# Rounding fp64 weights inside an attention + FFN kernel: the clamp on VectorE, a third of each weight while x arrives, the rest later

## Chip, cores, metric

One core of a Trainium2 chip. The metric is the device time of one execution in microseconds (us). Each time of a kernel below is a median of several executions with their range; what happens at which microsecond inside a kernel is read from its one profiled execution. PE is TensorE's matmuls, PEld its weight loads, DVE VectorE, ACT ScalarE, POOL GpSimd, SP SyncE.

## The reference, cut to what matters

```python
B, N, m, C = 4, 12416, 32, 128              # x [B,N,C] fp32, inducing points [m,C] fp32
h   = mab(inducing, x)                      # softmax(inducing x^T / sqrt(C)) x
att = mab(x, h)                             # each token of x attends to the 32 rows of h
xn  = att / rms(att) * rms_g                # 49664 tokens of 128
out = (silu(xn @ w_gate) * (xn @ w_val)) @ w_out      # d_ff = 1536; the weights are fp64
```

The three weights are fp64, 128 x 1536 words each. The kernel reads them as pairs of 32-bit words and rounds them to fp32 by integer steps: exponent out of the high word, clamped to what fp32 has, shifted into place; mantissa likewise; sign and low word joined in; one product. Each weight is cut into three chunks of 128 x 512, called (i,c): i = 0 gate, 1 val, 2 out; c = 0, 1, 2 the third.

## The kernel before

The FFN runs in slots of 128 hidden channels (12 slots make a unit of 512 tokens): gate matmul, val matmul, SiLU, multiply, and out projection two slots later. The next batch's attention is laid between the slots. Only batch 0's attention and the rounding of the weights stand ahead of the first slot; this part is called the head.

Some words for it. A *score group* is the scores of one piece of x against h. The FFN takes the attention weights themselves as input, so h is folded into the gate and val weights: a *stack* is the product of h with one third of such a weight, copied by ScalarE, with a subtraction on VectorE behind the copy. *gram* is the product of h with itself; from it comes each token's mean square. The *seam* is the chain that makes the attention weights of one piece ready for the FFN: product with gram, transposed back (z), reduced, the power (1/rms, on GpSimd), the scaling by it, a split into a high and a low part, and four small transfers (the gather).

The rounding of one chunk (cut):

```python
def load_w(i, c):
    ...
    def parts():
        ve.tensor_scalar(out=e[:], in0=high, scalar1=20, scalar2=0x7FF, op0=ALU.logical_shift_right, op1=ALU.bitwise_and)
        nc.gpsimd.tensor_scalar(out=e[:], in0=e[:], scalar1=896.0, scalar2=1151.0, op0=ALU.max, op1=ALU.min)   # the clamp, L211
        nc.scalar.activation(e[:], e[:], AF.Copy, bias=-896.0 * (1 << 23), scale=float(1 << 23))               # L212
        ve.tensor_scalar(out=f[:], in0=high, scalar1=0xFFFFF, scalar2=None, op0=ALU.bitwise_and)
        nc.scalar.activation(f.bitcast(F32)[:], f[:], AF.Copy, bias=1.0, scale=2.0 ** -20)                     # L214
    def join():
        ve.scalar_tensor_tensor(...)          # sign into e
        ve.scalar_tensor_tensor(...)          # low word into f
        nc.gpsimd.tensor_tensor(out=dst, in0=f.bitcast(F32)[:], in1=e.bitcast(F32)[:], op=ALU.mult)
        put()                                 # store the chunk for later batches, fetch the next raw chunk
```

The order of the work ahead of the first slot (cut); `convert` does the next half of a chunk:

```python
for s in range(NS):                    # 7 pieces of x
    for k in range(R): f["turn_x"](s, k)          # transposes; copies on ScalarE, each second one on VectorE
    if s: f["scores1"](s - 1); convert()
...
f["exp2"](0, 1); convert()
turn_a(); square()                     # square also turns z back
for i in range(2): f["stack_of"](i, 0) # matmul, ScalarE copy, VectorE subtraction
scale(); convert(3)
for c in range(1, NC):
    for i in range(2): f["stack_of"](i, c)
apply(); split(); gather(0, 0); convert(3)
# slots 0 and 1: the last two convert()
```

## Time and profile before

| | before |
|---|---|
| time, median of 4 (range) | 1759.96 us (1759.11 to 1761.65) |
| span of the profiled execution | 1759.6 us |
| PE, DVE, ACT, POOL busy | 97%, 65%, 44%, 11% |
| first FFN matmul | 83.05 us after the start |
| slot 9 starts | 103.33 us |

The first two rows are whole executions; the last two are read from the timeline of the profiled one. They matter because from about slot 9 on TensorE has hardly any gaps (from 118 us to the end it waits 4.3 us in all), so a microsecond won ahead of that slot is won at the end. The other views of this profile are shown in the prediction.

### The profile page before, as it was taken

What the parts mean: (1) busy time and instruction counts of PE and PEld (TensorE: products, weight loads), DVE (VectorE), ACT (ScalarE), POOL (GpSimd) and SP (SyncE); (2) the same over time, 40 slices, a digit from 0 to 9 for tenths busy, and PEclk for the clock granted to TensorE, in tenths of its full rate; (3) what the DMA queues carried; (4) which work ended last, traced back from release to release, by engine and by line L of the source; (5) the groups of instructions that cost most, each with busy time, mean ns of one, the idle gap of its engine ahead of it and who ended that gap; (6) DMA issues with size and microseconds to landing.
All of it is one profiled execution on the core that took longest, in us unless ns stands there. A gap on an engine that the chain in (4) does not pass through costs nothing.

```text
span 1759.6 us, 20237 instructions
## 1 busy us (share of the span) xinstructions
PE 1707.2 (97%) x6234; PEld 955.4 (54%) x6234; DVE 1144.2 (65%) x1982; ACT 769.0 (44%) x1288; POOL 188.4 (11%) x135
## 2 busy tenths in 40 slices
PE   6499999999999999999999999999999999999998
PEld 4245555555565555554556555555456555555555
DVE  4567765666567776566666777666656666666655
ACT  4244445333544444533454444534354444444444
POOL 2411100102111001011010010110101101100100
PEclk9699999999999999999999999999999999999999
DMA  6235363124343226113425315413211121121111
GB/s 252 66 67 86 54 144 68 42 66 75 56 76 67 51 54 147 36 42 90 69 51 90 54 30 112 100 28 80 49 31 36 28 42 25 31 42 33 27 35 23
DMA packets 389338, 112.44 MB, mean 64 GB/s; under 512 B 365136, under 2 KB 369776, under 8 KB 386672
## 3 DMA queue, kind: packets, MB, share of 16 engines
q1 hardware_dynamic: 388944, 111.02, 30.7%
q8 instruction: 49, 0.80, 0.2%
q14 instruction: 57, 0.47, 0.1%
q10 hardware_dynamic: 288, 0.15, 0.0%
HBM read 53.95 MB, written 27.00 MB: 46 GB/s over the span
## 4 chain that ended last, share of the span: by engine, by line
PE 92%; ACT 3%; DVE 2%; POOL 1%; issue 1%; DMA 1%; SPq 0%; DVEq 0%; ACTq 0%; POOLq 0%
PE acc L480 55%; PE gv L496 15%; PE gv L498 15%; PE mm L265 2%; PE mm L428 1%; PE mm L319 1%; ACT silu L500 1%; POOL u L211 1%; PE gv L265 1%; DMA xn<-in_x_dram 1%; ACT L500 1%; ACT sc L294 0%; PE gv L319 0%; ACT sc L367 0%; PE mm L380 0%
## 5 line engine op out<-in xcount | busy, mean ns | idle before, releaser
L480 PE MATMUL acc<-u,wo 128*128 128x512 f32 (+2 forms) x2400 | 1200.1, 583 | 0.3
L502 DVE TENSOR_TENSOR u<-silu,gv 128x512 f32<-128x512 f32 (+2 forms) x1200 | 798.5, 670 | 561.3 <-ACT silu L500 555.4
L500 ACT ACTIVATE silu<-gv 128x512 f32<-128x512 f32 (+2 forms) x1200 | 699.5, 584 | 926.7 <-DVE u L502 507.1
L496 PE MATMUL gv<-a,sg 128*128 128x512 f32 (+2 forms) x1200 | 922.4, 769 | 10.9 <-DMA a<-lo 8.1
L480 PEld LDWEIGHTS acc<-u,wo 128*128 128x128 f32 x2400 | 440.4, 188 | 151.0 <-issue 58.5
L498 PE MATMUL gv<-a,sv 128*128 128x512 f32 (+2 forms) x1200 | 465.8, 388 | 1.9 <-ACT silu L500 1.3
L496 PEld LDWEIGHTS gv<-a,sg 128*128 128x128 f32 x1200 | 227.5, 190 | 287.3 <-issue 272.4
L498 PEld LDWEIGHTS gv<-a,sv 128*128 128x128 f32 x1200 | 228.1, 190 | 275.4 <-issue 194.6
L431 POOL TENSOR_TENSOR z<-z,sc 128x512 f32<-128x512 f32 (+2 forms) x27 | 32.0, 1186 | 1043.3 <-DVE z L430 1022.8
L439 POOL TENSOR_TENSOR rs<-ms,mhalf 128x16 f32<-128x16 f32 (+2 forms) x28 | 75.9, 2711 | 116.6 <-DVE ms L437 116.6
L483 DVE STREAM_TRANSPOSE o<-acc 128x512 f32<-128x512 f32 (+2 forms) x100 | 69.1, 691 | 1.5 <-PE acc L480 1.1
L360 POOL TENSOR_TENSOR sc<-sc,mx 128x512 f32<-128x512 f32 (+2 forms) x24 | 23.2, 968 | 311.7 <-DVE mx L359 253.8
L245 DVE STREAM_TRANSPOSE xT<-xT 128x512 f32<-128x512 f32 (+2 forms) x84 | 53.2, 633 | 0.0
L428 PE MATMUL mm<-eT,gram 128*128 128x512 f32 (+2 forms) x56 | 28.4, 589 | 5.0 <-DVE eT L420 5.0
L443 POOL TENSOR_TENSOR sc<-sc,rs 128x512 f32<-128x512 f32 (+2 forms) x27 | 26.4, 976 | 2.1
L212 ACT ACTIVATE u<-u 128x512 int32<-128x512 int32 x9 | 5.7, 630 | 39.3 <-POOL u L211 39.3
L211 POOL TENSOR_SCALAR u<-u 128x512 int32<-128x512 int32 x9 | 18.2, 2018 | 35.3 <-DVE u L210 35.1
L253 PE MATMUL gv<-ident,xn 128*128 128x128 f32 x97 | 15.6, 326 | 5.9 <-ACT xT L259 3.5
L430 DVE STREAM_TRANSPOSE z<-mm 128x512 f32<-128x512 f32 (+2 forms) x28 | 18.6, 666 | 3.9 <-PE mm L428 3.9
L265 PE MATMUL mm<-xT,hT 128*32 128x512 f32 (+2 forms) x150 | 20.9, 592 | 0.0
L319 PE MATMUL mm<-xn,e 128*32 128x128 f32 x582 | 20.7, 276 | 0.0
L265 PE MATMUL mm<-xT,indT 128*32 128x512 f32 (+2 forms) x168 | 20.0, 547 | 0.0
(127 smaller groups left out, 445.5 us busy)
## 6 DMA issues: line engine op xcount, KB each, us to landing
out_dram<-o SPq DMA_DIRECT2D x320, 64.0 KB, 2.0
xT<-in_x_dram SPq DMA_DIRECT2D x60, 256.0 KB, 4.8
xn<-in_x_dram SPq DMA_DIRECT2D x60, 256.0 KB, 5.9
a<-hi SPq DMA_DIRECT2D x160, 64.0 KB, 2.0
a<-lo SPq DMA_DIRECT2D x158, 64.0 KB, 2.0
w<-w SPq DMA_DIRECT2D x21, 256.0 KB, 3.2
xn<-in_x_dram SPq DMA_DIRECT2D x5, 1024.0 KB, 11.6
out_dram<-o SPq DMA_DIRECT2D x64, 60.0 KB, 2.0
```

The lines of the kernel that those rows point to most:

```text
L211: nc.gpsimd.tensor_scalar(out=e[:], in0=e[:], scalar1=896.0, scalar2=1151.0, op0=ALU.max, op1=ALU.min)
L245: nc.vector.transpose(out=t[:, ts(k, n * m)], in_=t[:, ts(k, n * m)])
L265: nc.tensor.matmul(ps[ts(q, m), 0:w], lhsT, xT[b, s][:, ts(q, w)], start=True, stop=True)
L319: nc.tensor.matmul(ps[ts(t % R, m), 0:C], e[:, ts(t, m)], xn[:, t, :], start=head and t < R, stop=not more)
L428: nc.tensor.matmul(ps[rows, 0:w], gram[b][rows, rows], st["eT"][rows, 0:w], start=True, stop=True)
L439: nc.gpsimd.tensor_tensor(out=rs, in0=ms, in1=mhalf[rows, 0:n], op=ALU.pow)
L480: nc.tensor.matmul(acc[:, 0:T], wo[:, j, :], t[:, 0:T], start=(j == 0), stop=(j == NJ - 1))
L483: nc.vector.transpose(out=o[:, 0:T], in_=acc[:, 0:T])
L496: nc.tensor.matmul(g[:, 0:T], sg[:, ts(j, P)], a[:, 0:T], start=True, stop=True)
L498: nc.tensor.matmul(v[:, 0:T], sv[:, ts(j, P)], a[:, 0:T], start=True, stop=True)
L500: nc.scalar.activation(sl[:, 0:T], g[:, 0:T], AF.Silu)
L502: nc.vector.tensor_tensor(out=t[:, 0:T], in0=sl[:, 0:T], in1=v[:, 0:T], op=ALU.mult)
```

## The change

Intent: less work and fewer waits between engines ahead of the first slot. In parts:

1. The clamp goes from GpSimd to VectorE. While x arrives, the "place" steps (L212, L214) are done on VectorE too, and ScalarE has all copies of x.
2. Chunks are taken by thirds: only (0,0), (1,0), (2,0) while x arrives; (0,1), (1,1), (0,2) in gaps of the attention chain; (1,2), (2,1), (2,2) in slots 0 to 6.
3. Within the attention chain: scores against h ahead of the gram product, gram's copies on ScalarE, the stack's subtraction split from its copy and set behind the seam's reduction, the first FFN unit gathered before the stacks of the second third, the exponentials to h in four instructions instead of seven.
4. In the full part: some steps move by a few slots. Batch 0's remaining score groups begin seven slots later, so that by slot 9 one is done instead of three.

The core of the diff, cut:

```diff
-    chunks = [(i, c) for i in range(3) for c in range(NC)]
+    chunks = [(i, c) for c in range(NC) for i in ((0, 1, 2) if not c else (0, 1))] + [(2, c) for c in range(1, NC)]
...
-            nc.gpsimd.tensor_scalar(out=e[:], in0=e[:], scalar1=896.0, scalar2=1151.0, op0=ALU.max, op1=ALU.min)
+            nc.vector.tensor_scalar(out=e[:], in0=e[:], scalar1=896.0, scalar2=1151.0, op0=ALU.max, op1=ALU.min)
...
+        def place(scalar):
+            ...
+                    if scalar:
+                        nc.scalar.activation(to[:], t[:], AF.Copy, bias=add, scale=mul)
+                    else:
+                        nc.vector.tensor_scalar(out=to[:], in0=t[:], scalar1=mul, scalar2=add, op0=ALU.mult, op1=ALU.add)
...
-                if k == 1:
-                    nc.vector.tensor_copy(out=dst, in_=src)
-                else:
-                    nc.scalar.copy(out=dst, in_=src)
+                nc.scalar.copy(out=dst, in_=src)
...
+    early = [(step, i) for i in range(3) for step in (parts, join)]     # while x arrives: third 0
...
+    parts(1, 1)
+    place(1, 1)
     for i in range(2):
         f["stack_of"](i, 0)
+    turn_z()
     scale()
+    for i in range(2):
+        f["stack_low"](i, 0)
+    join(1, 1)
-    convert(3)
-    for c in range(1, NC):
-        for i in range(2):
-            f["stack_of"](i, c)
     apply()
     split()
     gather(0, 0)
+    parts(0, 2); place(0, 2)
+    for i in range(2):
+        f["stack_of"](i, 1); f["stack_low"](i, 1)
+    join(0, 2)
...
+            for k, step in enumerate((parts, place, join)):
+                add(k // 2, step, 1, NC - 1)                  # slots 0, 0, 1
+            for i in range(2):
+                add(2 + i, f["stack_of"], i, NC - 1)
+                add(2 + i, f["stack_low"], i, NC - 1)
+            for c in range(1, NC):
+                for k, step in enumerate((parts, place, join)):
+                    add(2 * c + 1 + k // 2, step, 2, c)       # slots 3, 3, 4 and 5, 5, 6
```

## The prediction

> **What bounds the kernel now.** I read the page first, then the stretches of the head, then the waits there, then the timeline around the two longest gaps. The page: slices of 44 us, then the chain that ended last.
>
> ```profile
> PE   6499999999999999999999999999999999999998
> PEclk9699999999999999999999999999999999999999
> ...
> PE 92%; ACT 3%; DVE 2%; POOL 1%; issue 1%; DMA 1%; SPq 0%; DVEq 0%; ACTq 0%; POOLq 0%
> ```
>
> TensorE is full from the third slice on, at full clock. From 118 us to the end its matmuls wait 4.3 us in all (the waits of PE in that window). That part is bound by TensorE's work, which the change leaves alone, so nearly all there is to win or lose lies in the two weak slices. Stretches of these (span, busy of PE, PEld, DVE, ACT, POOL; clock; DMA share; GB/s):
>
> ```profile
> 0.00:20.00 20.00, 11.96 (x65) 8.82 (x65) 5.56 (x19) 5.62 (x9) 2.79 (x8) 1.00 0.89 356
> 20.00:40.00 20.00, 11.37 (x92) 6.71 (x92) 11.20 (x30) 10.79 (x23) 8.96 (x6) 0.89 0.51 173
> 40.00:60.00 20.00, 12.53 (x210) 9.99 (x211) 13.28 (x32) 6.62 (x17) 6.47 (x5) 0.67 0.25 81
> 60.00:80.00 20.00, 8.62 (x12) 2.72 (x11) 12.67 (x24) 4.29 (x8) 7.91 (x5) 0.67 0.07 28
> 80.00:100.00 20.00, 13.57 (x41) 6.37 (x42) 11.69 (x18) 7.65 (x12) 8.78 (x6) 0.65 0.68 117
> 100.00:120.00 20.00, 20.00 (x76) 9.23 (x74) 13.41 (x22) 7.17 (x12) 4.15 (x4) 1.00 0.31 55
> ```
>
> From 20 to 90 us no engine is full: it is a chain from engine to engine. The waits of 0 to 60 and of 60 to 110 us (total, times, longest) name its link:
>
> ```profile
> ACT u L212 <- POOL u L211: 22.1, 6, 8.1
> ...
> ACT u L212 <- POOL u L211: 17.2, 3, 8.5
> PEld gv L394 <- POOL silu L220: 8.3, 2, 7.1
> ```
>
> L211 is the clamp in the rounding of a weight. ScalarE takes work in order, so its copies, exponentials and SiLUs stand behind L212, which waits for L211. The timeline shows the cost at the end of the head: normalisation power, ScalarE released late, the attention weights scaled (L443), the first FFN matmul, its first SiLU.
>
> ```profile
> 65.92 3.24 POOL L439 TENSOR_TENSOR rs<-ms,mhalf 128x16 f32<-128x16 f32 x1 [7.16 <-DVE ms L437]
> 72.43 0.63 ACT L212 ACTIVATE u<-u 128x512 int32<-128x512 int32 x1 [8.53 <-POOL u L211]
> 76.63 0.69 DVE L443 TENSOR_TENSOR sc<-sc,rs 128x512 f32<-128x512 f32 x1
> 83.05 0.77 PE L496 MATMUL gv<-a,sg 128*128 128x512 f32 x1 [8.13 <-DMA a<-lo]
> 87.82 1.09 ACT L500 ACTIVATE silu<-gv 128x512 f32<-128x512 f32 x2
> ```
>
> The power is ready at 69.16, but L443 starts at 76.63: VectorE's queue has the stack copies of all three thirds first, and these wait for ScalarE, which waits for POOL.
>
> **What the Trainium skill says.** (1) GPSIMD Engine Reference, section "4.1 Engine selection": elementwise work belongs on VectorE; it calls one-input operations on GpSimd roughly line-rate. The trace agrees with the advice, not with that rate: the clamp takes 2.02 us on POOL, a one-input operation of the same shape (L210) 0.42 us on DVE. (2) VectorE: DVE Perf Modes, "The perf-mode tier table (the rule you actually need)": one-input fp32 operations in SBUF run at twice the rate of two-input ones. Trace: 0.42 us (L210) against 0.68 (L218), so the clamp and the two "place" operations should cost DVE about 0.42 each, 0.34 in a row. (3) TensorE: Matmul & The Clock Gate, "Part 1: The HAM clock gate": an idle TensorE runs at half clock until it has been busy some 3.4 us. The trace agrees: 0.50 in 84 to 92 us, 0.77 in 92 to 96, 1.00 after. Fewer gaps mean less time cold, but each step after a gap stays cold.
>
> **The change, part by part.**
>
> (a) While x arrives. The last large piece of x lands at 23.7 us (issue plus landing time), the small rest at 24.4. Per 16-column piece PE needs 1.97 for transposes and 1.06 for scores. In the kernel before, the pieces wait for ScalarE behind the clamp and the last score (a reduction on DVE) ends at 36.3. Now all copies are on ScalarE (4 x 0.5 = 2.1 us per piece, under PE's 3.03) and the rounding runs on DVE alone: 5 x 0.34 = 1.7 us for parts and place, 1.3 for join. From 15.85, where PE warms up, four pairs of 3.0 end at 27.8. DVE then has: scores to 28.7, parts 30.4, scores 31.1, join 32.4, scores 32.7. The maximum starts at 32.75 instead of 36.35: **3.6 us won**.
>
> (b) Exponentials to h. The first exponential no longer stands behind L214: +0.6. The three part operations of chunk (0,1) end 1.05 after the bias, about when the exponential does, so the transpose of e starts at 35.8 instead of 39.9 (4.1 won). The 194 matmuls keep their 8.22 us. Then join (1.3) instead of parts (0.67) stands ahead of the reciprocal: 0.6 given back. hT at 47.6 instead of 51.1: **3.5 won so far**.
>
> (c) Scores against h. Today DVE waits for the gram memset behind POOL, copies gram (0.79) and joins (1.3) before the score transpose, 3.05 after hT. Now scores come first on PE and gram goes to ScalarE: 0.34 + 1.13 = 1.47 after hT. **5.1 won so far.**
>
> (d) The seam. Today the two stack subtractions (DVE waits for ScalarE's copies) come ahead of the reduction, which starts 4.7 after the z transpose; now 1.45. DVE has 1.35 of sums and 1.05 of parts while PE forms the gram product (2.05), so z keeps its place within 0.2. **8.2 won so far**: the power starts at 57.75 and ends at 60.95. Beside it DVE does two subtractions (1.4) and a join (1.3), the second subtraction gated by a ScalarE copy at about 59.0, ending near 61.0: just hidden. L443 starts at 61.05 instead of 76.63, **15.6 won**, of which 7.4 is the end of the wait after the power. From L443 to the first FFN matmul stays 6.4 us (split, DMA): 67.5 instead of 83.05. Parts (0,2) and the stacks of the second third lie in that DMA's shadow.
>
> (e) Given back in the first slots. A slot is 1.32 us of PE (0.23 + 0.2 + 0.86). ACT has the copies until 67.5 and the table load of 1.28, so SiLU 0 is at 68.8; DVE joins (0,2) to 69.5, then multiplies. Each of the three chunks left makes a ring of two slots: part (0.7 until the exponent is there), place on ScalarE (1.15), SiLU behind it (0.6), multiply (0.65), join (1.3), multiply (0.65) = 5.05 us against 2 x 1.32 on PE. For (1,2) POOL's product (1.28), two stack matmuls, a copy (0.6) and a subtraction (0.7) follow before DVE goes on. Followed through: multiply 1 at 73.3, product of (1,2) at 75.8, subtraction to 79.0, parts (2,1) to 80.0, multiply 4 at 82.1, parts (2,2) to 84.9, multiply 7 at 88.8, and slot 9 starts at 89.3. Without waits nine slots, a score group (1.06) and the stacks (1.7) would be 14.6 us; so 21.8 - 14.6 = **7.2 us are lost here**.
>
> (f) The kernel before loses here too: ScalarE is blocked until 86.5, then PE runs cold to 96; its slot 9 is at 103.30, with three score groups done where the new kernel has one (2 x 1.06 still to do). So 103.3 - 89.3 - 2.1 = **11.9 us won** when PE is full in both. After that the same work follows. Square ahead of turn_z saves DVE 3.9 us of waiting in 28 seams, but DVE is not the bound there; split three slots after scale in the first seam may cost half a us. I count both as nothing.
>
> Sum: 1760.1 - 11.9 = **1748 us**, a gain of 0.7%.
>
> **Rivals.** First, **the first slots hide the rounding**: DVE is only 65% busy over the span and ScalarE 44%. Then most of the 7.2 of (e) comes on top, a win of 18 to 19 and some 1741 us. Against it: the ring crosses engines, and in 88 to 96 us of the kernel before the same joins held DVE at 3.5 of 4 us. Second, **the wait moves**: DVE becomes the bound in slots 0 to 8 (5.9 multiplies, 3.2 parts, 3.9 joins, 1.4 subtractions = 14.4 us against PE's 11.9), PE gaps keep it cold, and longer rings give back most of the win: 5 or 6 us left, 1754 us. Third, **x was the bound anyway**: everything before 24.4 us is hidden under DMA (its share is 0.91 to 1.02 in every 4 us from 4 us on), so (a) could shrink to nothing if the DVE queue holds the last scores longer; the result would be 1751 to 1752. Fourth, the moved seams and turn steps stall PE in the full part; with 4.3 us of waits now, and DVE at some 65%, I give that at most 3 us.
>
> **Range and chances.** The terms of (b) to (d) are read from single instructions and should hold within 2 us together; (a) within 2; (e) within 4, the weakest. Together about 5: 1741 to 1754. A gain over 2% would need 35 us out of a head of 83 with a DMA floor of 24 and an 8.2 us matmul run: 1%. A loss over 2%: 1%.
>
> **What would show it.** In the changed profile: no wait of ScalarE on a POOL clamp; maximum near 32.8 us; power near 57.8; L443's counterpart at its end near 61; first FFN matmul near 67.5; slot 9 near 89, with DVE and ScalarE alternating in waits between 68 and 88; the clock at 1.00 from about 90. The prediction fails if the scores end well after 33 us, if L443 waits for ScalarE again, or if slot 9 comes before 84 or after 94.

## The result, and the profile after

| | before | after |
|---|---|---|
| time, median of 4 (range) | 1759.96 us (1759.11 to 1761.65) | 1751.48 us (1750.36 to 1751.72) |
| ratio (95% interval) | | 0.9949 (0.9932 to 0.9967) |
| span of the profiled execution | 1759.6 us | 1748.6 us |

A ratio here and below is the mean time of one kernel's runs over that of the other's of the same rounds, so it isn't quite the ratio of the medians. The gain is 8.5 us, 0.5%: small, but the interval excludes no change. 1748 was predicted, 1741 to 1754 the range.

The page after, the same three lines (slices of 44 us; chain that ended last): only the first two slices have moved, and little of that is visible at this grain.

```profile
PE   6699999999999999999999999999999999999998
PEclk9699999999999999999999999999999999999999
...
PE 92%; ACT 3%; DVE 3%; DMA 1%; issue 1%; POOL 0%; ACTq 0%; DVEq 0%; POOLq 0%
```

The stretches after (span, busy of PE, PEld, DVE, ACT, POOL; clock; DMA share; GB/s):

```profile
20.00:40.00 20.00, 13.78 (x165) 9.64 (x166) 13.98 (x36) 10.78 (x23) 3.72 (x3) 0.84 0.60 207
...
60.00:80.00 20.00, 14.85 (x26) 6.20 (x26) 14.44 (x25) 8.77 (x15) 4.18 (x3) 0.66 0.46 92
80.00:100.00 20.00, 17.23 (x60) 7.42 (x60) 14.62 (x23) 7.42 (x14) 4.65 (x4) 0.91 0.36 70
```

POOL falls from 8.96 to 3.72 us in 20 to 40, because the clamps are gone from it, and PE does 14.85 instead of 8.62 us in 60 to 80, because the FFN has begun. But 60 to 100 still has room: no engine is full there, and PE's granted clock is 0.66 in 60 to 80 and 0.91 in 80 to 100. The timeline after, in the same places as before: power, attention weights scaled, first FFN matmul, first SiLU.

```profile
56.68 2.92 POOL L464 TENSOR_TENSOR rs<-ms,mhalf 128x16 f32<-128x16 f32 x1 [10.02 <-DVE ms L462]
59.91 0.68 DVE L468 TENSOR_TENSOR sc<-sc,rs 128x512 f32<-128x512 f32 x1
65.58 0.77 PE L521 MATMUL gv<-a,sg 128*128 128x512 f32 x1 [1.73 <-DMA a<-lo]
67.47 0.60 ACT L525 ACTIVATE silu<-gv 128x512 f32<-128x512 f32 x1
```

The scaling now starts 0.3 us after the power ends (56.68 + 2.92), where it had started 7.5 us after. The first matmul is 17.5 us earlier than before, and the first SiLU 20.4. Slot 9, however, starts at 89.99 instead of 103.33: 13.3 us earlier, and with one score group done where the old kernel had three. Its gate matmul, first of the kernel before, then of this one:

```profile
103.33 0.80 PE L496 MATMUL gv<-a,sg 128*128 128x512 f32 x1
```

```profile
89.99 0.80 PE L521 MATMUL gv<-a,sg 128*128 128x512 f32 x1
```

What happens in the first slots is seen in the waits of 60 to 110 us and in the timeline of 78 to 85 us, when TensorE is in slots 5 and 6:

```profile
DVE u L527 <- ACT silu L525: 11.0, 10, 1.4
ACT u L221 <- DVE u L213: 7.7, 3, 3.6
```

```profile
78.53 0.43 DVE L213 TENSOR_SCALAR u<-u 128x512 int32<-128x512 int32 x1
...
78.99 0.63 ACT L221 ACTIVATE u<-u 128x512 int32<-128x512 int32 x1 [1.68 <-DVE u L213]
...
80.05 1.06 ACT L525 ACTIVATE silu<-gv 128x512 f32<-128x512 f32 x2
80.66 0.69 DVE L527 TENSOR_TENSOR u<-silu,gv 128x512 f32<-128x512 f32 x1 [1.36 <-ACT silu L525]
...
82.63 1.27 POOL L232 TENSOR_TENSOR wo<-o,u 128x512 f32<-128x512 f32 x1 [7.12 <-DVE o L230]
...
83.95 1.32 PE L505 MATMUL acc<-u,wo 128*128 128x512 f32 x2 [2.29 <-POOL wo L232]
```

This is the ring of chunk (2,1): ScalarE waits for VectorE's clamp (L213), its SiLU stands behind the place step (L221), VectorE's multiply (L527) waits for that SiLU, the join comes behind the multiply, and at last TensorE waits 2.29 us for POOL's product, because the out projection of slot 4 reads this chunk. The last line is one that my prediction did not have.

### The profile page after: what moved, and what is told of

Its sections match the earlier page's. It is cut to its first block, busy times and chain, and to the rows that moved or that the text cites. A ratio compares the mean times of both kernels' runs of the same rounds, so it can differ in the third digit from the quotient of the medians.

```text
span 1748.6 us, 20258 instructions
## 1 busy us (share of the span) xinstructions
PE 1706.9 (98%) x6234; PEld 954.8 (55%) x6234; DVE 1145.3 (65%) x1987; ACT 767.7 (44%) x1286; POOL 170.1 (10%) x126
## 4 chain that ended last, share of the span: by engine, by line
PE 92%; ACT 3%; DVE 3%; DMA 1%; issue 1%; POOL 0%; ACTq 0%; DVEq 0%; POOLq 0%
PE acc L505 56%; PE gv L521 15%; PE gv L523 15%; PE mm L275 2%; PE mm L450 1%; PE mm L332 1%; DMA xn<-in_x_dram 1%; ACT silu L525 1%; ACT sc L304 1%; PE gv L332 0%; ACT L525 0%; DVE u L527 0%; PE mm L398 0%; PE gv L266 0%; ACT sc L385 0%
## 5 line engine op out<-in xcount | busy, mean ns | idle before, releaser
L527 DVE TENSOR_TENSOR u<-silu,gv 128x512 f32<-128x512 f32 (+2 forms) x1200 | 798.7, 670 | 558.9 <-ACT silu L525 553.1
L450 PE MATMUL mm<-eT,gram 128*128 128x512 f32 (+2 forms) x56 | 27.8, 578 | 3.2 <-DVE eT L440 3.2
L275 PE MATMUL mm<-xT,hT 128*32 128x512 f32 (+2 forms) x192 | 26.8, 591 | 0.0
L468 POOL TENSOR_TENSOR sc<-sc,rs 128x512 f32<-128x512 f32 (+2 forms) x27 | 26.3, 975 | 2.1
L320 DVE STREAM_TRANSPOSE e<-sc 128x512 f32<-128x512 f32 (+2 forms) x28 | 17.7, 633 | 2.7 <-PE gv L332 1.8
L472 DVE STREAM_TRANSPOSE aT<-sc 128x512 f32<-128x512 f32 (+2 forms) x28 | 18.5, 660 | 1.2 <-POOL sc L468 1.2
L332 PEld LDWEIGHTS mm<-xn,e 128*32 128x32 f32 x582 | 15.0, 109 | 7.7 <-PE gv L521 5.5
L475 DVE TENSOR_TENSOR lo<-aT,hi 128x512 fp32r<-128x512 f32 (+2 forms) x28 | 18.1, 648 | 1.0
## 6 DMA issues: line engine op xcount, KB each, us to landing
xn<-in_x_dram SPq DMA_DIRECT2D x5, 1024.0 KB, 11.9
```

Source lines behind the costliest of these rows:

```text
L275: nc.tensor.matmul(ps[ts(q, m), 0:w], lhsT, xT[b, s][:, ts(q, w)], start=True, stop=True)
L332: nc.tensor.matmul(ps[ts(t % R, m), 0:C], e[:, ts(t, m)], xn[:, t, :], start=head and t < R, stop=not more)
L450: nc.tensor.matmul(ps[rows, 0:w], gram[b][rows, rows], st["eT"][rows, 0:w], start=True, stop=True)
L527: nc.vector.tensor_tensor(out=t[:, 0:T], in0=sl[:, 0:T], in1=v[:, 0:T], op=ALU.mult)
```

## The experiments

All are edits of the changed kernel unless said otherwise. Times were taken in rounds with the kernel before on the same chip: e1 to e8 on one, e9 to e11 on another, where the kernel before was 0.3 to 0.6 us slower (median 1760.37 against 1759.76 and 1760.03). Differences between medians of the two groups are uncertain by that much.

My theory: the gain is made ahead of the first slot, by the clamp's engine and the order of the work together, and part is given back in a ring between VectorE and ScalarE in the first slots. Rivals: the order alone or the clamp alone does it; a cold TensorE or the moved slots of the full part eat the rest.

### The two kernels once more: e1_after_again and e9_before_again

No edit.

> The changed kernel unaltered, timed again beside the kernel before, because the first ratio (0.9949, interval 0.9932 to 0.9967) is wide against a gain of 0.5%. The two profiled executions differ by 11.0 us (1759.6 against 1748.6), the medians by 8.5. If the account of the head is whole (slot 9 of the FFN reached 11.2 us earlier once two score groups of 1.06 us still to do are taken off), the ratio should come out near 0.9940 (10 to 11 us). If something after slot 9 eats part of it in most executions, it stays near 0.9952 (8.5 us).

Measured: 1751.14 us (1750.43 to 1752.81, 5 runs) against 1759.76 (1758.92 to 1761.59): ratio 0.9950 (0.9938 to 0.9963). So 8.6 us, not 10 or 11.

> The kernel before unaltered, for a second trace. The trace of before that I predicted from belongs to an execution of 1761.65 us, 1.9 above the median of its ten (1760.03). If the slow extra lies in the head, slot 9 starts near 101.4 here instead of 103.3 in an execution of about 1760, and the change's gain at slot 9 is 9.3 us instead of 11.2, which is what the medians show (8.7). If slot 9 is at 103.3 again, 2 us of the gain are lost elsewhere. The ratio itself: 1.000.

Measured: 1761.06 us (1760.65 to 1761.76, 4 runs), ratio 1.0003. The expectation failed in part: the profiled execution took 1760.98, not about 1760, and its slot 9 started at 102.74 instead of 103.33, 0.59 us of the 0.67 by which it was faster than the execution I had predicted from. In the two profiled executions of e9 and e1 the gain at slot 9 is 102.74 - 2 x 1.06 - 90.09 = 10.5 us, and their times differ by 1760.98 - 1750.66 = 10.3. The trace of a pair is thus explained whole by its head. The medians differ by less than the profiled executions, 8.6 us against 10.3 here and 8.5 against 11.3 in the first pair, because the profiled executions of before (1761.65, 1760.98) lie above its medians in the rounds (1759.76 to 1760.37) and those of after (1750.36, 1750.66) below its own (1751.48, 1751.14). What is different in the head of a 1759 us execution no trace here shows; that stays open.

### Which half of the change makes the gain: e2_clamp_on_pool and e3_before_clamp_dve

```diff
-            nc.vector.tensor_scalar(out=e[:], in0=e[:], scalar1=896.0, ...)
+            nc.gpsimd.tensor_scalar(out=e[:], in0=e[:], scalar1=896.0, ...)
```

> One line of the changed kernel: the clamp of a weight's exponent goes back to GpSimd (2.02 us there, 0.42 on VectorE). My theory, that the chain through GpSimd was the cost: while x arrives the two place operations on VectorE wait for it, about 1.6 us at the last chunk; chunk (0,2) frees ScalarE about 1.2 us later ahead of the first SiLU; each of the three rings in the first slots grows by about 1.6. Together some 7 us: about 1758, most of the gain gone. Rival, that the order of the work and not the clamp's engine makes the gain: 0 to 3 us, at most 1754.

Measured: 1758.18 us (1758.12 to 1760.51), ratio 0.9994 (0.9981 to 1.0006) to before. Of 8.6 us, 7.0 are gone: as my theory had it. The waits of this kernel, first of 0 to 60 and then of 60 to 110 us:

```profile
DVE u L223 <- POOL u L213: 5.4, 3, 1.8
...
ACT u L221 <- POOL u L213: 12.6, 3, 5.2
```

VectorE waits three times 1.8 us at most for the clamp while x arrives, and the rings of the first slots stretch. The first matmul is only 1.6 us late (67.22), slot 9 is 7.5 late (97.45).

The other way round, the kernel before with the clamp on VectorE:

```diff
-            nc.gpsimd.tensor_scalar(out=e[:], in0=e[:], scalar1=896.0, ...)
+            ve.tensor_scalar(out=e[:], in0=e[:], scalar1=896.0, ...)
```

> One line of the kernel before: the clamp goes from GpSimd to VectorE, the order of the work stays. My theory: ScalarE is freed earlier while x arrives (2 to 3 us), ahead of the stack copies (1.6) and ahead of the first SiLU (3.3): 6 to 8 us in all, about 1753, so that the clamp's engine alone gives most of what the whole change gives. Rival, that the new order is needed for the gain: 2 us or less, 1758 or more.

Measured: 1757.07 us (1754.81 to 1758.3), ratio 0.9980 (0.9966 to 0.9993). Between both: 2.7 us in the medians, where I expected 6 to 8. The timeline of this kernel shows what I had overlooked:

```profile
68.49 2.08 PE L394 MATMUL gv<-silu,hg 128*128 128x512 f32 x2 [6.05 <-POOL silu L220]
...
74.44 0.69 DVE L443 TENSOR_TENSOR sc<-sc,rs 128x512 f32<-128x512 f32 x1
```

Without the clamp ScalarE is free, but the product of chunk (1,1) still stands behind the power on POOL; the stack matmul waits 6.05 us for it, and L443 still comes behind all stacks: it is earlier by 2.2 us, about what x's arrival gave (the maximum starts at 34.27 instead of 36.35). So neither half does it alone: the clamp's engine 2.7 us, the order with the clamp left on POOL 1.6 us in the medians (the interval includes no change), both together 8.6. Which of the moves within the order gives how much, no run here separates.

### What the first slots cost: e4_no_slot_rounding

```diff
-            for k, step in enumerate((parts, place, join)):
-                add(k // 2, step, 1, NC - 1)
+            add(1, borrow)          # val's last third := gate's last third (wrong on purpose)
...
-            for c in range(1, NC): ...       # no (2,1), (2,2)
-            nc.tensor.matmul(acc[:, 0:T], wo[:, j, :], t ...
+            nc.tensor.matmul(acc[:, 0:T], wo[:, j % 4, :], t ...
```

> The changed kernel without any rounding in the FFN slots: the chunks (1,2), (2,1) and (2,2) aren't rounded; w_val's last third uses w_gate's, and the out projection uses its first third for all; the result is wrong on purpose. Slots 0 to 8 took 24.4 us in the changed kernel where 14.6 would do without waits. My theory, that the rings of part, place, SiLU, multiply, join cause the 9.8 us: some 7 us of them come back (the table load of 1.28 and the filling of the pipeline stay), about 1744. Rival, that a cold TensorE (clock 0.50 in 64 to 72 us) or the DMA of the first attention weights causes them: 3 us or less, 1748 or more.

Measured: 1743.8 us (1743.34 to 1744.11), ratio 0.9907; the result is wrong, as meant. 7.3 us below the changed kernel, and slot 9 at 82.64 is 7.35 earlier. So the rounding of three chunks in the first slots costs 7.3 us; the first matmul, at 65.83, hadn't moved.

### Is it the ring or the sum of the work: e5_relay

```diff
             for k, step in enumerate((parts, place, join)):
-                add(k // 2, step, 1, NC - 1)
+                add(k, step, 1, NC - 1)
+                add(2 + k, step, 2, 1)
+                add(6 + k, step, 2, 2)
             for i in range(2):
-                add(2 + i, f["stack_of"], i, NC - 1)
-                add(2 + i, f["stack_low"], i, NC - 1)
-            for c in range(1, NC): ...
+                add(3 + i, f["stack_of"], i, NC - 1)
+                add(3 + i, f["stack_low"], i, NC - 1)
```

> The changed kernel with the three chunks of the first slots spread: each chunk's parts, place and join stand in three slots after one another (0,1,2 for (1,2); 2,3,4 for (2,1); 6,7,8 for (2,2)), the stacks of the last third in slots 3 and 4. ScalarE's place then follows a SiLU that is already there and doesn't wait for VectorE's parts. My theory, that the ring between the engines costs the time: 4 to 6 us less than the changed kernel, about 1746. Rival, that VectorE's sum of work (13.6 us in eight slots against PE's 12.3) is the bound there: 2 us or less, since the work is the same.

Measured: 1746.45 us (1745.97 to 1746.56), ratio 0.9921 (0.9906 to 0.9937): 4.7 us below the changed kernel, with the same instructions. Slot 9 is at 85.40. Its ScalarE at chunk (2,2):

```profile
83.29 0.63 ACT L221 ACTIVATE u<-u 128x512 int32<-128x512 int32 x1 [0.29 <-DVE u L213]
83.82 0.61 ACT L221 ACTIVATE o<-o 128x512 f32<-128x512 int32 x1
84.34 0.58 ACT L525 ACTIVATE silu<-gv 128x512 f32<-128x512 f32 x1
```

The wait for VectorE is 0.29 us instead of the 3.62 that the same step has in the changed kernel. The ring, not the sum of the work, was the larger part of the cost. What is shown is the worth of the whole new placing: the edit also sets the stacks one slot later, starts (2,1) one slot earlier and (2,2) one later. TensorE's wait of 2.29 us for the product of (2,1) is gone in it; that for the product of (1,2) is 2.12 instead of 1.20.

This kernel also shows a collision between VectorE and GpSimd at the scaling of the attention weights:

```profile
59.59 1.26 POOL L232 TENSOR_TENSOR silu<-o,u 128x512 f32<-128x512 f32 x1
59.64 1.76 DVE L468 TENSOR_TENSOR sc<-sc,rs 128x512 f32<-128x512 f32 x1
```

In the changed kernel L468 takes 0.68 us and POOL's product beside it 1.64; here POOL begins 0.05 us ahead, takes 1.26, and L468 takes 1.76, as if it could begin only after POOL had ended. The Trainium skill says why, SBUF — State Buffer, section "SBUF: two separate sides": VectorE and GpSimd share a port pair under an exclusive lock held for the whole instruction, and when the VectorE operation has two inputs in SBUF, as here, whoever starts first makes the other wait. The two traces agree, in both directions. It moved the first matmul of this kernel to 66.36, 0.8 us later than in the changed one, so the relay gained in spite of it. It isn't the relay's doing: e8, whose head is the changed kernel's, has it too (1.78 us, first matmul at 66.30), and e4. In e5 and e8 the join that feeds POOL's product ended some 0.5 us sooner (59.51 in e5, 60.00 in the changed kernel), so that POOL went on to the product as soon as the power was done and came first.

### Is it the cold TensorE: e6_warm_pe

```diff
+    dummy = ps_acc.tile([P, 512], F32, name="acc")
+    for _ in range(4):
+        nc.tensor.matmul(dummy[:], ident[:], xT[0, 0][:, 0:512], start=True, stop=True)
     turn_z()
     ...
+    for _ in range(2):        # the same matmul, behind the stacks of the second third
```

> The changed kernel with six additional matmuls without use (each two passes of 0.43 us cold) in TensorE's gaps at 58 to 62 and 64 to 65.5 us, to see whether the half clock in 64 to 72 us costs time. My theory, that the ring of the engines bounds these slots: the clock rises earlier, the time falls by 0 to 2 us. Rival, that cold matmuls (1.42 for 0.80, 1.91 for 1.02) are most of the 9.8 us lost: 4 us or more less.

Measured: 1750.63 us (1750.55 to 1751.16), ratio 0.9947 (0.9933 to 0.9960): 0.5 us below the changed kernel, inside the spread. The stretch of 64 to 68 us of the changed kernel, then that of this one and the two after it (clock third from the end):

```profile
64.00:68.00 4.00, 2.27 (x4) 1.07 (x4) 2.27 (x4) 3.92 (x6) 0.00 (x0) 0.50 0.20 49
```

```profile
64.00:68.00 4.00, 2.52 (x6) 0.67 (x4) 2.12 (x5) 3.71 (x6) 0.00 (x0) 1.00 0.20 50
68.00:72.00 4.00, 3.41 (x5) 1.53 (x6) 2.91 (x5) 1.60 (x4) 1.27 (x1) 0.55 0.21 67
72.00:76.00 4.00, 2.80 (x6) 1.04 (x5) 3.60 (x6) 1.87 (x4) 1.27 (x1) 0.59 0.98 155
```

The dummies did warm the clock, from 0.50 to 1.00 in 64 to 68 us, and slot 9 stayed where it was: 90.17 against 89.99. So the cold start of the first two slots costs nothing. But the clock fell again at once: the two matmul forms that the rival names still take 1.42 and 1.92 us at 72.74 and 71.81. The later cold stretches are not tested by this run, and the traces must decide. In the changed kernel TensorE is cold and without gaps from 69.10 to 74.37, but then waits for POOL's product of (1,2) in any case (1.20 us, to 75.56), and no matmul in that stretch feeds this product. From 83.95 to slot 9 it has no gaps either, at a clock of 0.59 in 84 to 88, and takes 6.04 us for the matmuls that took 4.29 in e5 at 1.00. My estimate from these two: up to 1.7 us of the 9.8 are a cold TensorE, behind the wait for POOL's product of (2,1). They go with that wait, as in e5; apart from it they were not tested.

### The time in which x arrives: e7_x_window and e10_late_fetch

While x arrives, parts and join of (2,0) stand in VectorE's queue ahead of the last two score reductions. The changed kernel:

```profile
28.13 0.42 DVE L211 TENSOR_SCALAR u<-sc 128x512 int32<-128x512 int32 x1
...
29.94 0.65 DVE L279 TENSOR_SCALAR_CACHE_REDUCE sc<-gv 128x480 f32<-128x480 f32 x1
...
31.98 0.16 DVE L284 TENSOR_REDUCE mx<-gmx 128x1 f32<-128x7 f32 x1
```

```diff
-    early = [(step, i) for i in range(3) for step in (parts, join)]
+    early = [(step, i) for i in range(2) for step in (parts, join)]
     for s in range(NS):
         f["turn_e"](s)
+        if s + 1 == NS: place(0, 1); place(2, 0); join(0, 1)
         f["sum_h"](s)
+        if s == 3: parts(2, 0)
     ...
     place(0, 2)
+    join(2, 0)                # and its mantissa tile from another pool, chunks fetched in this order
```

> The changed kernel with chunk (2,0) taken out of the time in which x arrives: its parts and place go into the long matmul run of h, its join behind the split of the attention weights; the join of (0,1) goes ahead of the copy of h. The last two score reductions waited for VectorE behind parts and join of (2,0): the maximum started at 31.98 and could start at 29.9; the reciprocal no longer waits 0.6 us for a join. My theory: 2 to 2.6 us less, first FFN matmul near 63, and the same gain at the end, about 1749. Rival, that x's arrival and TensorE's transposes bound it anyway: 0.5 us or less.

Measured: 1747.73 us (1747.02 to 1749.91), ratio 0.9933 (0.9920 to 0.9945): 3.4 us below the changed kernel. The maximum starts at 29.61 (2.4 earlier), the power at 53.13 (3.55 earlier), as hoped and a little more; but the first matmul not at 63:

```profile
56.36 0.69 DVE L469 TENSOR_TENSOR sc<-sc,rs 128x512 f32<-128x512 f32 x1
...
58.62 0.39 SPq L180 DMA_DIRECT2D sg<-in_moe_w_out_dram  x1
...
64.38 0.77 PE L522 MATMUL gv<-a,sg 128*128 128x512 f32 x1 [4.08 <-DMA a<-lo]
```

From scaling to first matmul takes 8.0 us here, 5.7 in the changed kernel. The new fact is the raw fetch (L180, 512 KB) that my edit had set just ahead of the four small transfers of the attention weights. e10 fetches it behind them:

```diff
-            if unread:
+            if unread and (i, c) != (1, 1):
                 fetch_raw(*unread.pop(0))
```

> As e7_x_window, but the fetch of the last raw chunk is moved behind the small transfers of the first attention weights. In e7 the attention weights were scaled at 56.36, 3.6 us before the changed kernel's 59.91, but the first FFN matmul was at 64.38, only 1.2 us before its 65.58: a raw fetch of 512 KB was issued 0.5 us ahead of them. My theory: they landed behind that fetch; without it the first FFN matmul starts near 62.1 and the time falls by 1 to 2.3 us below e7 (1747.7), to about 1746. Rival, that something else holds them (ScalarE's issue, VectorE's cast): no change.

Measured: 1746.81 us (1746.71 to 1748.19), ratio 0.9925 (0.9911 to 0.9938).

```profile
61.76 0.77 PE L522 MATMUL gv<-a,sg 128*128 128x512 f32 x1 [1.75 <-DMA a<-lo]
```

The small transfers land in 2.1 to 2.3 us instead of 4.2 to 4.6, those issued by ScalarE as well as those by SyncE, and the first matmul is at 61.76. That settles the fetch as the cause. Of these 2.6 us only 0.7 reach slot 9 (86.24 against 86.95). The medians differ by 0.9, but e7 and e10 ran on different chips and their intervals overlap, so a gain in time isn't shown. Where the other 1.9 us go in the first slots, no run here separates.

### The moved slots of the full part: e8_old_slots

```diff
-                at = 20 + 14 * s if b else 38 + 12 * s
+                at = 20 + 14 * s
-                add(at + 14, g["scores1"], s)
+                add(at + 16, g["scores1"], s)
-                j = ((14, 14, 17, 18, 21, 21, 33) if k else ...
+                j = ((14, 14, 18, 18, 21, 21, 33) if k else ...
```

> The changed kernel with the steady slots of the kernel before: transposes and scores of the next batch at 20+14s and 16 later, square in the slot of turn_z for every seam but the first. I counted these moves as nothing: within 1.5 us of the changed kernel. Rival: the gain in the median (8.5) is smaller than that at slot 9 (11.2) because the moved slots cost TensorE time in the full part; then this is 2 to 3 us faster than the changed kernel.

Measured: 1751.51 us (1751.21 to 1751.9), ratio 0.9951 (0.9938 to 0.9965): the same as the changed kernel. The moves that this edit takes back are worth nothing either way.

### The findings together: e11_best

```diff
+  # relay in the first slots, stacks of the last third in slots 4 and 5
+  # (2,0) out of the time in which x arrives, late fetch
-                j = (... (29, 29, 31, 31, 33, 33, 36))[i]
+                j = (... (29, 29, 31, 31, 33, 33, 38))[i]     # the first seam's split, two slots later
```

> Relay in the first slots (stacks of the last third in slots 4 and 5), chunk (2,0) out of the time in which x arrives, the late fetch, and the first seam's split two slots later (a wait of 1.14 us of TensorE on the multiply behind it). If the gains add: 1751.1 - 4.7 (relay) - 5 (window with late fetch) - 1 (split) = about 1740.5. If the first slots have a floor of their own (VectorE's sum), the parts overlap and it is 1743 or more.

Measured: 1741.29 us (1739.72 to 1741.68, 4 runs), correct, ratio 0.9888 (0.9875 to 0.9902) to the kernel before: 19 us below it, 10 below the changed kernel (timed on the other chip). Alone, relay (4.7) and window with late fetch (4.3) give 9.0, so the gains add, to within 1 us. The split wasn't timed alone; its wait of 1.14 us is gone from the trace, in which TensorE's longest wait for that multiply is 0.2. Slot 9 starts at 79.78.

One table shows that the head explains all of them. Slot 9 is read from the one profiled execution of each; for the two kernels in the old order, which have done two more score groups by then, 2.1 us are taken off.

| kernel | first FFN matmul | slot 9 | median |
|---|---|---|---|
| before (e9) | 82.96 | 102.74 - 2.1 = 100.6 | 1761.06 |
| clamp on DVE, old order (e3) | 80.92 | 98.89 - 2.1 = 96.8 | 1757.07 |
| clamp on POOL, new order (e2) | 67.22 | 97.45 | 1758.18 |
| changed (e1) | 65.67 | 90.09 | 1751.14 |
| old slots in the full part (e8) | 66.30 | 90.29 | 1751.51 |
| warm PE (e6) | 65.79 | 90.17 | 1750.63 |
| x window (e7) | 64.38 | 86.95 | 1747.73 |
| x window, late fetch (e10) | 61.76 | 86.24 | 1746.81 |
| relay (e5) | 66.36 | 85.40 | 1746.45 |
| no slot rounding, wrong result (e4) | 65.83 | 82.64 | 1743.80 |
| together (e11) | 61.76 | 79.78 | 1741.29 |

The median follows slot 9 to within a microsecond or so, and does not follow the first matmul: e2 and the changed kernel start within 1.6 us of one another and end 7.0 apart. From slot 9 to the last gate matmul the traces of before and after need the same: 1752.05 - 103.33 = 1648.7 us, and 1740.98 - 89.99 - 2.1 = 1648.9.

## Why the prediction was right, and where its terms were off

The time fell inside the range, near its slow half (1751.5 for 1748), and it was right for the stated reason. None of its three signs of failure came: the scores ended at 31.9 us, the scaling waited for VectorE's join and not for ScalarE, slot 9 was at 89.99. That 1748 wasn't further off is partly luck, as two of its errors nearly cancelled (f). By its own steps:

- **What bounds the kernel.** Held: the part after slot 9 is the same to 0.2 us in both traces, and in all eleven runs the median follows slot 9 to about a microsecond.
- **(a) x's arrival.** Maximum at 32.75 predicted, 31.98 measured. TensorE warmed up one piece of x earlier than I assumed (the first eight score matmuls, from 12.96, take 1.06 us together, before the third piece had come; in the kernel before they took 1.47). The scores of the last large piece ended at 27.44 on TensorE instead of 27.8, about half of the 0.8. That VectorE's queue, with parts and join of (2,0), holds the last scores was in the sum, and e7 confirms it as worth 2.4 us.
- **(b) to (d), the chain to the scaling.** Power predicted at 57.75, measured 56.68; scaling 61.05 against 59.91. After the 0.8 of (a) the rest is off by 0.3, but two errors within it nearly cancel: hT was at 46.30 instead of 47.6, 0.5 more than (a) explains, and from there the score transpose took 1.84 instead of 1.47. The clamp costs VectorE 0.43 us, as worked out from L210.
- **First matmul.** 67.5 predicted, 65.58 measured: the way from the scaling through the split and its transfers took 5.7 us where before had 6.4.
- **(e) the first slots.** The mis-sized term. 7.2 us lost were predicted; measured from 65.58 to 89.99 are 24.4 us, so 24.4 - 14.6 = 9.8. The ring was right in kind (e4, e5); e6 excludes the cold clock of the first two slots alone. Missing from it were the wait for POOL's product of (2,1) by the out projection, 2.29 us at 83.95, and two blocks of VectorE's first part step by POOL's products (1.00 at 68.97 and 1.11 at 83.06 instead of 0.42, each ending 0.3 us after the product), and the cold clock behind the first of these waits, up to 1.7 by the estimate under e6. A slot's three terms there, 0.23 + 0.2 + 0.86, add up to 1.29; the 1.32 that was used is what the traces have from gate to gate. e4 puts the whole cost of rounding there at 7.3 us; some 2.2 of the 9.8 stay without it (16.8 us from first matmul to slot 9 in e4).
- **(f) and the sum.** The win at slot 9 was predicted as 11.9; it is 103.33 - 89.99 - 2.1 = 11.2 in the pair of traces I had, 10.5 in e9 and e1. The early start (1.9) and the longer slots (2.6) nearly cancelled, which is luck. The rest of the difference to 8.5 is that the trace I predicted from was an execution at the slow end of its kernel (1761.65, median 1760) while its win was taken off the median, and that the trace after was at the fast end (1750.36, median 1751.5).
- **Small terms.** The first seam's split, guessed at half a us, held TensorE for 1.14. The moves that e8 took back are nothing, as counted.

One belief of mine fell. I expected the clamp alone, in the old order, to give 6 to 8 us; it gave 2.7, because POOL's product stood behind the power and the scaling behind the stacks (e3). The gain belongs to both halves together.

## What to carry to other kernels

When a prologue is a chain over in-order engines, move a slow link and the order around it together: here either alone gave 1.6 (not clear of noise) or 2.7 us, both 8.6. Work pushed behind the start isn't free because the engines have room on average; look for steps of different in-order engines that wait for one another within a slot. Here setting three dependent steps of a chunk in three slots instead of two, with the stacks moved to suit, gave 4.7 us with the same instructions. And judge such a change where the bound engine becomes full, not where it starts.

## What the Trainium skill lacked or had wrong

- GPSIMD Engine Reference, "4.1 Engine selection": it calls one-input operations on GpSimd roughly line-rate. The int32 clamp of 128x512 took 2.02 us on GpSimd (1.92 to 2.15) and 0.43 us on VectorE: 4.7 times.
- TensorE: Matmul & The Clock Gate, "Why this matters for your kernels": it advises against idle gaps of TensorE of more than about 3 us. Dummy matmuls that filled two gaps (3.5 and 1.7 us) raised the clock from 0.50 to 1.00 in 64 to 68 us and changed the time by 0.5 us of 1751, within the spread; the page lacks a word on stretches in which TensorE waits for other engines anyway.
- No page that I read has a number for small transfers behind a large one: four of 64 KB, issued 0.5 to 1.3 us after a fetch of 512 KB, landed in 4.2 to 4.6 us instead of 2.1 to 2.3, from ScalarE's queue as well as from SyncE's.
- SBUF — State Buffer, "SBUF: two separate sides", was right about the lock; what the order of the program doesn't tell is who gets it. The same scaling of 128x512 took 0.68 us in one kernel and 1.76 in another in which POOL began 0.05 us ahead of it.
